# A smaller cap on the bytes of the first loads, and one weight piece finished by halves

## The chip, the cores and the metric

The kernel runs on one core of one Trainium2 chip. The number that counts is the device time of one execution in microseconds (us), as a median over runs. In the text PE is TensorE, DVE is VectorE, ACT is ScalarE, POOL is GpSimd and SP is SyncE, which here only starts DMA transfers. "PEq", "SPq" and so on are the sequencers of these engines.

## The reference

Two steps are computed, one behind the other. The first is a retention layer: for 8 batches and 8 heads, with 576 positions and a head dimension of 64, the scores are multiplied by a decay and a causal mask, with no softmax. The second is a feed-forward block over the 4608 tokens, 512 to 2048 to 512, with a PReLU between.

```python
scores = scale * np.matmul(q, k.transpose(0, 1, 3, 2))
Dmat = np.where(rel >= 0, gamma[:, None, None] ** rel[None, :, :], 0.0)
attn = np.matmul(scores * Dmat[None], v)          # (8, 8, 576, 64)
x = attn.transpose(0, 2, 1, 3).reshape(4608, 512)
h = x @ w_in                                      # (4608, 2048)
g = np.maximum(h, 0.0) + alpha * np.minimum(h, 0.0)
out = (g @ w_out).astype(np.float32)
```

q, k and v are 4-byte floats in HBM. The two weight matrices lie there as 8-byte floats, because they are multiplied by a double when they are set up; each is 1M elements, 8 MB. The kernel turns them into 4-byte floats itself.

## The kernel before, in words

**Blocks.** The feed-forward block works on blocks of 256 tokens (18 of them, numbered kb) and 8 units i of 256 hidden columns. A unit first makes ph = w_in' x (PE, `plain_unit` L419 for the first two blocks, `mlp_unit` L463 for the others), then the activation g (ACT and DVE), then adds g w_out to the sums po (PE, L398 and L381). The first two blocks (`PLAIN`) use plain products, while the weights are still arriving; the other 16 use a scheme with seven products in the place of eight.

**Weights.** Each weight matrix comes in 16 pieces of 512 KB, in the order two of w_in, two of w_out, two of w_in and so on (`pieces`). In `fetch` a piece of w_in is loaded by two DMAs of 256 KB, a piece of w_out by one of 512 KB, through `load` on SP's queue (L78). `piece_in` (L285) starts the conversion on ACT: `a` is the absolute value of the upper halves (L296), and the lower halves are scaled in place (L298). `piece_out` (L301) ends it: three DVE operations on 128x512 elements, clamp (L307), shift and mask (L310), sign (L312), and one POOL operation that adds the lower halves (L314).

**The cap.** `load` keeps a list of the loads asked for so far. A load waits until an earlier one has landed, chosen so that the bytes asked for after that one, with its own, come to at least `in_flight[0]`. The value is 5 << 18 (five times 256 KB, 1.25 MB) at the beginning and 7 << 18 after part one of the first batch has been asked for; later it is 0, which is no cap. SP takes its DMAs in order, so a load that waits holds all behind it.

**The first batch.** Batch 0 goes in three parts of 4, 4 and 1 chunks of 64 positions (`PARTS`). Part 0 is six transfers of 256 KB: k, q and v, each in two halves; its q goes over ACT's queue and isn't counted by the cap (L161). `part_transposes` (PE L697), `part_scores` (PE L716, DVE L723), `part_states` (PE L736, ACT L744, POOL L746) and `part_values` (PE L764 and L775) make the first 256 columns of x; three ACT copies for each half of them (L781, L783) bring them into `xb[0]`, and after those the first unit can start. All this is written out by hand, one call after the other, in a scheduling scope that keeps the order on each engine:

```python
fetch(6)
load_part(1)
in_flight[0] = 7 << 18
fetch(8)
...
piece_in(1)
part_states(0)
piece_in(2)
piece_out(2)
part_carry(0)
part_values(0)
...
piece_in(2)
piece_out(1)
part_scale(1, 1)
plain_unit(0, 0)
```

So on ACT the conversion of pieces 0, 1 and 2 (numbered from 0; piece 2 is the first of w_out) stands ahead of the copies into `xb[0]`. The steps below call the loads k0, k1, v0, v1 (part 0), w0 to w7 (the pieces, with a and b for two halves), k0' to v1' (part 1). The first unit's 16 matmul instructions go through the four blocks of 128 columns of x, cc = 0 to 3: cc 0 and 1 need piece 0, cc 2 and 3 need piece 1.

Of the kernel before, what the change touches and what calls it, by code (L numbers as in the profile page):

```python
# [10 lines left out]
FP32 = mybir.dt.float32  # L11
INT32 = mybir.dt.int32
UINT32 = mybir.dt.uint32
ACTF = mybir.ActivationFunctionType
ALU = mybir.AluOpType
# [3 lines left out]
def kernel(  # L19
# [10 lines left out]
    nc = tc.nc  # L30
# [3 lines left out]
    P = 128  # L34
# [9 lines left out]
    HM = DM // 2  # L44
# [42 lines left out]
                ahead += n  # L87
            flight.append((ins, size))

    in_flight = [5 << 18]  # L90

# [99 lines left out]
    for i in range(NBIT - 1):  # L193
        nc.vector.scalar_tensor_tensor(out=dif[:, i + 1], in0=dif[:, i], scalar=2.0,
                                       in1=dif[:, i], op0=ALU.add, op1=ALU.mult)
# [6 lines left out]
                            op=ALU.mult)  # L202
    nc.vector.tensor_scalar(pf, pf, 1.0, None, ALU.add)

    for o, x, y in ((slice(0, 2), slice(0, 2), slice(3, 5)), (0, 0, 1), (0, 0, 2), (1, 0, 5)):
# [7 lines left out]
                                   in1=pf[:, 6], op0=ALU.mult, op1=ALU.mult)  # L213
# [17 lines left out]
    for h2 in range(2):  # L231
# [6 lines left out]
                                       in1=tabx[hd, :, 0], op0=ALU.add, op1=ALU.mult)  # L238
# [13 lines left out]
    HI_MAX = float(np.array([0x47EFFFFF], np.uint32).view(np.float32)[0])  # L252
    HI_MIN = float(np.array([0x38000000], np.uint32).view(np.float32)[0])
# [10 lines left out]
    def fetch(n):  # L264
        while npiece[0] < min(n, len(pieces)):
            srcs, at = pieces[npiece[0]][0], npiece[0]
            npiece[0] += 1
            free[:] = [t for t in free if at < gone.get(t, len(pieces))]
            t = free.pop(0)
            if isinstance(t, str):  # L270
                raw = ring.tile([P, 4 * HM], INT32, tag=t, name=f"raw_{at}")
            else:
                raw = w_in[t][:, 4:6].rearrange("p s u c f -> p (s u c f)").bitcast(INT32)
            for i, src in enumerate(srcs):
                to = raw
                if len(srcs) > 1:
                    to = raw.rearrange("p (x e f two) -> p x e f two", x=2, e=2, two=2)[:, :, i]
                load(to, src, P * 4 * HM * 4 // len(srcs))
            raws.append((raw, t))
# [21 lines left out]
    def piece_out(n):  # L301
        for _ in range(min(n, len(half_done))):
            at, a, lo, hi, t = half_done.pop(0)
            dst = pieces[at][1]

            c = ps_h.tile([P, 2, HM], INT32, tag="psh1", name=f"wc_{at}")
            nc.vector.tensor_scalar(c.bitcast(FP32), a, HI_MIN, HI_MAX, ALU.max, ALU.min)  # L307


            nc.vector.tensor_scalar(c, c, 3, 0x3FFFFFF8,  # L310
                                    ALU.logical_shift_left, ALU.bitwise_and)
            nc.vector.scalar_tensor_tensor(out=dst.bitcast(INT32), in0=hi, scalar=-0x40000000,  # L312
                                           in1=c, op0=ALU.bitwise_and, op1=ALU.bitwise_or)
            nc.gpsimd.tensor_tensor(out=dst.bitcast(INT32), in0=dst.bitcast(INT32), in1=lo,  # L314
                                    op=ALU.add)
            free.append(t)
            fetch(at + 1 + AHEAD)

# [517 lines left out]
# [5 lines that stand above are left out]
    aps = ps_a.tile([P, NFC], FP32, tag="psa", name="aps")  # L841
    nc.tensor.transpose(aps, a16, ident[0:NFC, 0:NFC])
    piece_out(1)
    nc.vector.tensor_copy(alpha, aps)
    nc.vector.tensor_scalar(nalpha, alpha, -1.0, None, ALU.mult)
# [4 lines that stand above are left out]
# [97 lines left out]
    for b in range(2, B):  # L947


        nq, first, at = len(queue), b * NPAIR, {}  # L950
# [56 lines left out]
```

## Time and profile before

| | |
|---|---|
| time, median of 3 runs | 1020.53 us (1019.59 to 1022.61) |
| span of the profiled execution | 1018.5 us |
| PE busy | 1001.3 us, 98% |
| PE weight loads busy | 894.2 us, 88% |
| DVE, ACT, POOL busy | 778.3, 269.4, 179.2 us |
| first matmul of the first unit | 19.26 us after the start of the span |
| DMA share in the first 25 us | 9 tenths of all 16 engines |

PE works without a rest from the second slice of 25 us to the end, so a time that PE loses or wins near the start is found again at the end of the span. The first slice is the only one in which PE is busy for 6 tenths only, and the only one with a granted clock under 9 tenths. The change touches only what happens there. In the views that follow, an entry such as "[0.76 <-POOL w_in L314]" says how long the engine was idle before the entry and what released it.

### The profile page before, as it was taken

To read this page: it belongs to the slowest core of one execution; us is meant where nothing else is said; L and a number is where in the kernel's file an instruction comes from. 1 tells how busy PE (TensorE), PEld (TensorE's weight loads), DVE (VectorE), ACT (ScalarE), POOL (GpSimd) and SP (SyncE) were. 2 spreads that over 40 slices of the span, in tenths; PEclk is the share of its full clock that TensorE was granted. 3 is DMA by queue.
4 is the path that set the end of the run, shared out by engine and by line. 5 is a ranking of instruction groups with operands and counts; after the bars stand their busy time and mean duration, and the time that the engine had idled before them with its cause. 6 is when DMAs were issued, how large, how long until landed. Compare 5 with 4: busy or idle time off the path is not lost.

```text
span 1018.5 us, 23084 instructions
## 1 busy us (share of the span) xinstructions
PE 1001.3 (98%) x9385; PEld 894.2 (88%) x9385; DVE 778.3 (76%) x2086; ACT 269.4 (26%) x605; POOL 179.2 (18%) x201
## 2 busy tenths in 40 slices
PE   6999999999999999999999999999999999999997
PEld 5666668899999999999999999999999999999997
DVE  6669966878887888768778788887878777667665
ACT  4556653223222222122021312232222211000000
POOL 5656674300100020100010000200020001010000
PEclk8999999999999999999999999999999999999999
DMA  9975744322231323112112313222313000000000
GB/s 238 238 194 140 185 74 103 60 60 48 52 64 40 63 37 69 25 45 48 44 25 56 60 45 60 57 48 54 62 45 60 13 23 1 22 1 21 2 21 22
DMA packets 229308, 64.30 MB, mean 63 GB/s; under 512 B 214337, under 2 KB 222545, under 8 KB 229201
## 3 DMA queue, kind: packets, MB, share of 16 engines
q1 hardware_dynamic: 227088, 62.29, 27.1%
q8 instruction: 74, 1.21, 0.5%
q10 hardware_dynamic: 2112, 0.53, 0.3%
q14 instruction: 34, 0.27, 0.1%
HBM read 53.35 MB, written 9.44 MB: 62 GB/s over the span
## 4 chain that ended last, share of the span: by engine, by line
PE 94%; DVE 3%; DMA 1%; ACT 0%; issue 0%; SPq 0%; POOL 0%; DVEq 0%; ACTq 0%
PE ph L463 38%; PE po L381 37%; PE ph L419 6%; PE po L398 6%; PE pv L656 3%; PE ps L614 1%; PE ps L620 1%; DMA w_out<-in_k_dram 1%; PE ph L614 1%; DVE su L589 0%; DVE g L476 0%; PE pt L697 0%; DVE mt L636 0%; PE ps L716 0%; PE ps L556 0%
## 5 line engine op out<-in xcount | busy, mean ns | idle before, releaser
L381 PE MATMUL po<-w_out,g 128*128 128x256 f32 x1792 | 410.9, 381 | 0.2
L381 PEld LDWEIGHTS po<-w_out,g 128*128 128x128 f32 x1792 | 330.1, 190 | 42.7 <-DVE g L487 1.3
L476 DVE TENSOR_TENSOR g<-ph,g 128x256 f32<-128x256 f32 (+1 forms) x512 | 187.0, 386 | 127.2 <-ACT g L471 75.2
L463 PE MATMUL ph<-xb,w_in 128*128 128x128 f32 x2048 | 272.7, 276 | 0.0
L463 PEld LDWEIGHTS ph<-xb,w_in 128*128 128x128 f32 x2048 | 257.1, 192 | 7.9 <-issue 0.7
L463 PE MATMUL ph<-xt,w_in 128*128 128x128 f32 x1536 | 213.8, 275 | 0.7 <-DVE g L476 0.7
L463 PEld LDWEIGHTS ph<-xt,w_in 128*128 128x128 f32 x1536 | 192.2, 192 | 1.1 <-PE ph L463 0.8
L487 DVE TENSOR_TENSOR g<-g 128x128 f32<-128x128 f32 x512 | 127.2, 289 | 5.4
L471 ACT COPY g<-ph 128x128 f32<-128x128 f32 x128 | 34.1, 266 | 327.7 <-PE ph L463 217.1
L528 POOL TENSOR_TENSOR qx<-qx,tabx 128x576 f32<-128x576 f32 x28 | 32.3, 1153 | 379.6 <-DMA qx<-in_q_dram 223.4
L481 DVE SCALAR_TENSOR_TENSOR g<-g 128x512 f32<-128x512 f32 x128 | 91.3, 714 | 3.8
L479 DVE TENSOR_SCALAR g<-g,alpha 128x256 f32<-128x256 f32 x256 | 84.3, 370 | 2.8
L597 ACT COPY vn<-su 64x512 f32<-64x512 f32 x56 | 34.6, 617 | 135.2 <-DVE su L591 134.5
L419 PE MATMUL ph<-xb,w_in 128*128 128x256 f32 x256 | 61.7, 397 | 0.8 <-POOL w_in L314 0.8
L419 PEld LDWEIGHTS ph<-xb,w_in 128*128 128x128 f32 x256 | 50.1, 198 | 11.0 <-issue 2.4
L398 PE MATMUL po<-w_out,g 128*128 128x512 f32 x128 | 58.6, 599 | 0.9 <-DVE g L435 0.9
L625 DVE SCALAR_TENSOR_TENSOR mt<-ph,th,mask 64x64 f32<-64x64 f32 x48 | 13.6, 283 | 52.5 <-PE ph L614 52.2
L665 ACT COPY xb<-pv 128x256 f32<-128x256 f32 (+3 forms) x84 | 22.7, 321 | 109.8 <-PE pv L656 109.8
L636 DVE SCALAR_TENSOR_TENSOR mt<-ps,th,mask 64x256 f32<-64x256 f32 x96 | 46.1, 481 | 2.3
L533 ACT ACTIVATE vn<-vn,tabv 64x576 f32<-64x576 f32 x56 | 43.3, 774 | 8.7 <-DMA vn<-in_v_dram 7.8
L398 PEld LDWEIGHTS po<-w_out,g 128*128 128x128 f32 x128 | 23.4, 190 | 24.5 <-issue 22.9
L589 DVE SCALAR_TENSOR_TENSOR su<-su,gch 128x64 f32<-128x64 f32 x84 | 43.1, 513 | 2.1
(134 smaller groups left out, 717.0 us busy)
## 6 DMA issues: line engine op xcount, KB each, us to landing
out_dram<-osb SPq DMA_DIRECT2D x36, 256.0 KB, 2.3
kx<-in_k_dram SPq DMA_DIRECT2D x112, 72.0 KB, 2.6
qx<-in_q_dram SPq DMA_DIRECT2D x112, 72.0 KB, 3.0
vn<-in_v_dram SPq DMA_DIRECT2D x56, 144.0 KB, 3.2
kn<-in_k_dram SPq DMA_DIRECT2D x56, 144.0 KB, 3.3
raw<-in_moe_w_in_dram SPq DMA_DIRECT2D x24, 256.0 KB, 4.5
raw<-in_moe_w_out_dram SPq DMA_DIRECT2D x10, 512.0 KB, 5.4
w_in<-in_moe_w_out_dram SPq DMA_DIRECT2D x6, 512.0 KB, 5.7
```

Of the source, the lines that this page charges most:

```text
L381: nc.tensor.matmul(acc[kb][n // 2][:, n % 2, :], g[:, x, :], w_out[i][:, y, :], start=(i == 0 and n % 2 == 0), stop=(i == NU - 1 and (n % ...
L398: nc.tensor.matmul(acc[kb][m], g[:, 2 * x + m], w_out[i][:, 2 * x:2 * x + 2].rearrange("p x f -> p (x f)"), start=(i == 0 and x == 0), sto ...
L419: nc.tensor.matmul(ph[:, x], w_in[i // UST][:, cc // 2 * 2 + x, i % UST, cc % 2], xb[kb][:, cc], start=(cc == 0 and x == 0), stop=(cc == N ...
L463: nc.tensor.matmul(ph[m][:, o], w_in[i // UST][:, l, i % UST, cc], r[:, cc], start=(n in (0, 3) and cc == 0), stop=(n in (2, 6) and cc == ...
L476: nc.vector.tensor_tensor(out=o, in0=x0, in1=x1, op=ALU.add)
L479: nc.vector.tensor_scalar(g[:, 4 + 2 * m:6 + 2 * m], g[:, 2 * m:2 * m + 2], 0.0, alpha[:, fc:fc + 1], ALU.min, ALU.mult)
L481: nc.vector.scalar_tensor_tensor(out=g[:, 0:4].rearrange("p x t -> p (x t)"), in0=g[:, 0:4].rearrange("p x t -> p (x t)"), scalar=0.0, in1 ...
L487: ins = nc.vector.tensor_tensor(out=g[:, o, :], in0=g[:, x0, :], in1=g[:, x1, :], op=op)
L533: nc.scalar.activation(vn[x, h2], vn[x, h2], ACTF.Copy, scale=tabv[x, c:c + 1])
L589: nc.vector.scalar_tensor_tensor(out=su[:, j], in0=su[:, j - 2], scalar=g2, in1=su[:, j], op0=ALU.mult, op1=ALU.add)
L597: nc.scalar.copy(vn[half(h2), h2, 1:], su[half(h2)])
L636: nc.vector.scalar_tensor_tensor(out=mt[to, h2, p2:NJ - 1:2], in0=ps[p2][half(x), 0], scalar=th[to, 3, h:h + 1], in1=mask[to, None, :].to_ ...
```

## The change

Two edits. The first makes the cap smaller while the first two parts of q, k and v and pieces 0 to 5 are asked for: 0.75 MB in the place of 1.25 MB; from piece 6 and part 2 on the cap is 1.75 MB as before. It is for having less queued in the DMA engines at the time when the first matmuls run. The second edit lets `piece_out` finish piece 1 in two halves of columns (cc = 2, then cc = 3), so that the first half's POOL addition does not wait for the second half's DVE work.

```diff
-    in_flight = [5 << 18]
+    in_flight = [3 << 18]
...
-            nc.vector.tensor_scalar(c.bitcast(FP32), a, HI_MIN, HI_MAX, ALU.max, ALU.min)
...
-            nc.vector.tensor_scalar(c, c, 3, 0x3FFFFFF8,
-                                    ALU.logical_shift_left, ALU.bitwise_and)
-            nc.vector.scalar_tensor_tensor(out=dst.bitcast(INT32), in0=hi, scalar=-0x40000000,
-                                           in1=c, op0=ALU.bitwise_and, op1=ALU.bitwise_or)
-            nc.gpsimd.tensor_tensor(out=dst.bitcast(INT32), in0=dst.bitcast(INT32), in1=lo,
-                                    op=ALU.add)
+            for f in (slice(0, P), slice(P, HM)) if at == 1 else (slice(0, HM),):
+                dst_e, c_e, a_e, hi_e, lo_e = [y[:, :, f] for y in (dst, c, a, hi, lo)]
...
+                nc.vector.tensor_scalar(c_e.bitcast(FP32), a_e, HI_MIN, HI_MAX, ALU.max, ALU.min)
...
+                nc.vector.tensor_scalar(c_e, c_e, 3, 0x3FFFFFF8,
+                                        ALU.logical_shift_left, ALU.bitwise_and)
+                nc.vector.scalar_tensor_tensor(out=dst_e.bitcast(INT32), in0=hi_e,
+                                               scalar=-0x40000000, in1=c_e,
+                                               op0=ALU.bitwise_and, op1=ALU.bitwise_or)
+                nc.gpsimd.tensor_tensor(out=dst_e.bitcast(INT32), in0=dst_e.bitcast(INT32),
+                                        in1=lo_e, op=ALU.add)
```

The order of the instructions on every engine stays as it was, but for three more on DVE and one more on POOL in piece 1; in the first unit PE gets a wait of its own ahead of cc = 3.

## The prediction, before the changed kernel ran

> **What bounds the kernel now.** I read the page first: busy shares, slices, the chain that ended last.
>
> ```profile
> PE   6999999999999999999999999999999999999997
> PEclk8999999999999999999999999999999999999999
> PE 94%; DVE 3%; DMA 1%; ACT 0%; issue 0%; SPq 0%; POOL 0%; DVEq 0%; ACTq 0%
> ```
>
> PE is 94% of the chain and full from slice 2 on. What the change can give is the distance by which the first dense unit ends earlier, if PE then finds its next inputs. So I read PE, ACT and SP over the first 30 us (start, duration, engine and line, idle before and its releaser).
>
> ```profile
> 12.90 0.33 PE L764 MATMUL pv<-pa,w_out 64*64 64x64 f32 x2
> 13.50 1.15 PE L764 MATMUL pv<-pa,w_out 64*64 64x64 f32 x62 [0.27 <-DVE pa L723]
> 14.58 0.42 PE L775 MATMUL pv<-pT,w_out 64*32 64x64 f32 x14
> 17.13 1.21 PE L775 MATMUL pv<-pT,w_out 64*32 64x64 f32 x82 [2.13 <-issue]
> 19.26 6.74 PE L419 MATMUL ph<-xb,w_in 128*128 128x256 f32 x16 [0.76 <-POOL w_in L314]
> ```
>
> Two things cost PE time here. In the middle of one group of L775, with no new operand, PE stands for 2.13 us and nothing released it ("issue"). And the first unit takes 6.74 us, where a later one of 16 takes 3.45 us in the chain of waits (58.89, 65.78). The windows view shows why (busy times, then the clock as the third number from the end):
>
> ```profile
> 11.80:18.60 6.80, 4.29 (x237) 3.65 (x230) 6.06 (x10) 5.30 (x12) 4.16 (x5) 1.00 0.94 303
> 18.60:25.40 6.80, 6.14 (x15) 4.92 (x16) 3.72 (x7) 3.95 (x9) 4.58 (x5) 0.50 0.99 233
> ```
>
> The trace's clock record: full from 11.79, half from 18.62, full from 25.45.
>
> The releaser named for the first unit is piece 1's POOL addition (17.89 to 19.17). But cc 0 and 1 need piece 0, done at 17.31, and xb, whose first half ACT finishes at 18.37 + 0.74 = 19.11. ACT's copies bind:
>
> ```profile
> 15.28 0.67 ACT L296 ACTIVATE wa<-w_in 128x512 f32<-128x512 f32 x1
> 15.84 0.66 ACT L298 ACTIVATE w_in<-w_in 128x512 int32<-128x512 uint32 x1
> 17.96 0.37 ACT L781 COPY xb<-pv 128x256 f32<-128x256 f32 x1 [1.47 <-PE pv L775]
> 18.37 0.74 ACT L783 COPY xb<-pv 64x256 f32<-64x256 f32 x2
> ```
>
> ACT is free at 16.50 and waits 1.47 us for PE's delayed L775. So the "issue" gap sets the start.
>
> **What the gap is.** PE's instruction records stop at number 449, and again at 1217 for 0.76 us in the same line. The difference is 768. The DMA packets of q8 (74 of 16,384 bytes, 1.21 MB, PE's instructions by their number) show one at 14.79 lasting 0.96, then PE goes on 1.38 us after its end; one at 38.08 lasting 1.02, PE on at 40.59, 1.49 us after it. [...] If the request comes on entering the block before (instruction 193, about 12.1 us; 961, about 34.2), the fetch waited 2.7 us under the cap of 1.25 MB and 3.8 us under 1.75 MB before its packet started.
>
> [...] those of 4096 bytes take about 0.18 us, those of 1024 about 0.05. [...] A wait behind all that is queued fits both fetches: 1.25 MB at some 300 GB/s is 4.2 us; less about 1.1 us from issue to first byte (k0: 0.80 to 1.91) [...], 2.3 are left; for 1.75 MB, 3.9. Both are near the observed waits, though the request times are inferred.
>
> **The cap's part.** For 0.75 MB the same sum is 2.6 - 1.9 = 0.7 us, at most 1.5 where two 512 KB loads overlap. From the packet records, whose 4-byte packets are semaphore writes, I take the landings before: k0 4.04, k1 6.32, v0 8.30, v1 9.49, w0a 10.44, w0b 11.19, w1a 11.94, w1b 12.69, w2 14.79, w3 16.74, k1' 22.6, q0' 23.7, q1' 24.7, v1' 27.4. SP answers a landing in 0.56 us:
>
> ```profile
> 11.00 0.35 SPq L78 DMA_DIRECT2D w_in<-in_moe_w_out_dram  x1
> 12.50 0.35 SPq L78 DMA_DIRECT2D raw<-in_moe_w_out_dram  x1
> 13.20 3.27 SPq L78 DMA_DIRECT2D raw<-in_moe_w_in_dram  x4
> ```
>
> With 0.75 MB: v1 waits for k0, and its first byte, 4.04 + 0.56 + 1.1 = 5.7, is still ahead of its turn at 8.08: no loss. w0a waits for k1, w0b for v0 (8.30 + 1.66 = 9.96, turn at 10.21): no loss. w1a waits for v1: 11.15 against 10.96. w1b: about 12.1, landed 13.1 against 12.69; ACT takes it at 14.05: no cost. w2 waits for w1a (landed 12.15): first byte 13.8, 1.5 us for 512 KB at 350 GB/s, landed about 15.9, 1.1 later than before.
>
> PE: at 12.1 only w1 is under way, so the instruction block arrives before 14.8 or within 0.7 us of it. The remaining 82 instructions need POOL's sums (14.49, 15.26), so L775 ends near 16.3 in the place of 18.34.
>
> ACT: its activation for piece 2 now waits for w2, 15.9 for 15.28, and with both activations done (1.22 us by the rows) is at 17.15. The first half of xb then takes 0.37 + 0.74 and is there at 18.25. The first unit starts at about 18.4, 0.86 us earlier. So of the 2.13 us of the gap, less than half comes through; the new wait for w2 takes the rest.
>
> **The clock.** [...] 25.45 - 18.62 is 6.83, [...] I estimate that the half clock costs about 1.7 us after (3.4 us at half) against 2.5 before (5 us), 0.8 less. The first unit would then end 0.86 + 0.8 = 1.7 us earlier.
>
> **What later loads take.** Part 1 goes three loads at a time and lands later by my count: k1' 23.7, q0' 25.0, q1' 26.2, v1' 28.8. Needed before at: k' 25.84 (L697), q' 24.53 (POOL L677), transposes of q' 29.58, v' 31.48. With 1.7 us less, k' is in time (24.1), q' scaled by 27.2 against 27.9: in time. v' in time (29.8). Nothing is lost up to some 2 us.
>
> **The halves.** DVE: three operations of 0.69 to 0.70 us become six on 128x256; nearest rows L479 0.370 and L435 0.476 (128x256), so 1.2 for each half, 2.4 against 2.16. The first addition on POOL then runs at once after piece 0's (17.31 to about 18.0; L746 at this size 0.73), the second ends near 18.75 in the place of 19.17. PE reaches cc 2 at 18.4 + 1.7 (eight at full clock), and the second half of xb is there at 19.4. So the halves are worth nothing unless the unit starts before 17.5; their 0.25 us on DVE lies beside PE's first unit. Zero.
>
> Sum: 1020.5 - 1.7 = 1018.8.
>
> **Rivals.** B: the clock never drops, because PE stands for 2.1 us between 16.3 and 18.4 and no longer for 2.1 and 0.8. The first unit then ends at 22.0, 4.0 us earlier, but k1' (23.7), q1' (26.2) and the v' scaling hold PE back; 2.5 to 4 us are left: about 1017. For it: fewer gaps; against: 63% of 11.79 to 18.62 was busy when it dropped, about 64% after. C: the fetch does not depend on the bytes queued; L775 starts at 17.13 as before and the time is 1020.3, less nothing but noise. For it: the request times are inferred, [...]. D, on the slow side: loads one by one leave the DMA engines idle (0.75 MB per 1.1 + 0.8 + 0.56 us and the transfer is 246 GB/s, where 1 KB packets ran at 350), so w2, part 1 and piece 6 come 2 to 4 us later than counted and PE waits for them: 1024. Against: k, q and v move at only 220 GB/s, which three in flight can still feed.
>
> **Numbers.** Mine 0.44, B 0.28, C 0.18, D 0.10. Faster by over 0.3% (3.06 us, under 1017.5) is most of B and the edge of mine: 0.28. Slower is D: 0.10. Within: 0.62. The range leaves out D and the far end of B: 1015.8 to 1021.4.
>
> **What would show it.** Right: the idle "issue" before L775 falls under 0.7 us; ACT's L296 on piece 2 waits for a DMA; the first L419 starts at 18 to 18.7; windows show the half clock for 3 to 4 us of the unit. Wrong: an unchanged 2.1 us gap (C); L697 or L677 waiting for part 1 for over 1 us (D); a first unit of 3.6 us (B).

## The result, and the profile after

| | before | after |
|---|---|---|
| median | 1019.78 us (6 runs, 1019.16 to 1022.61) | 1025.32 us (6 runs, 1023.50 to 1026.99) |
| ratio | | 1.0052, 95% interval 1.0036 to 1.0067 |
| span of the profiled execution | 1018.5 us | 1021.8 us |

The change costs half a per cent, some 5.3 us. The profiled execution after is the fastest of its six, so its trace shows 3.3 us of it. PE's timeline of the changed kernel over the first 38 us (start, duration, operation, idle before and releaser; lines behind L314 have moved on by four, so L775 is L779 here and L419 is L423):

```profile
14.40 0.42 PE L779 MATMUL pv<-pT,w_out 64*32 64x64 f32 x14
16.57 1.21 PE L779 MATMUL pv<-pT,w_out 64*32 64x64 f32 x82 [1.76 <-issue]
17.71 0.23 PE L846 MATMUL aps<-ident,a 16*128 16x16 f32 x1
19.95 6.17 PE L423 MATMUL ph<-xb,w_in 128*128 128x256 f32 x16 [2.01 <-POOL w_out L756]
27.39 0.63 PE L701 MATMUL pt<-ident,w_out 128*128 128x128 f32 x4 [1.27 <-DMA w_out<-in_k_dram]
28.44 0.63 PE L701 MATMUL pt<-ident,w_out 128*128 128x128 f32 x4 [0.42 <-DMA w_out<-in_k_dram]
...
31.66 0.66 PE L701 MATMUL pt<-ident,w_out 128*128 128x128 f32 x4 [0.43 <-POOL w_out L681]
...
37.74 3.29 PE L423 MATMUL ph<-xb,w_in 128*128 128x256 f32 x14 [1.06 <-issue]
```

The gap named "issue" before L779 is still there, 1.76 us for 2.13. The first unit starts 0.69 us later, not earlier. Then come waits that the kernel before doesn't have: twice for part 1's k, once for part 1's q (the POOL scaling L681 ahead of the transposes waits for its DMA), and a new "issue" gap in the middle of a unit.

What releases the first unit is named as a POOL operation, 19.31 to 19.92, that writes another tensor; ACT's copies into the block of x tell more:

```profile
17.58 0.67 ACT L296 ACTIVATE wa<-w_in 128x512 f32<-128x512 f32 x1 [1.44 <-DMA w_in<-in_moe_w_out_dram]
18.15 0.65 ACT L298 ACTIVATE w_in<-w_in 128x512 int32<-128x512 uint32 x1
18.70 0.35 ACT L785 COPY xb<-pv 128x256 f32<-128x256 f32 x1
19.06 0.74 ACT L787 COPY xb<-pv 64x256 f32<-64x256 f32 x2
```

Before, ACT waited for PE here; now it stands 1.44 us for w2's DMA, while the operands of its copies have been ready since PE's L779 ended at 17.78. The first half of x is there at 19.80, and the unit's first weight load follows 0.12 us later, as it did before (19.11 and 19.23).

The windows view shows what stands behind the DMA waits, in its last two columns (share of the 16 DMA engines, GB/s). The kernel before, then after:

```profile
10.00:20.00 10.00, 6.83 (x292) 6.02 (x292) 8.12 (x13) 6.68 (x16) 6.64 (x8) 0.93 0.96 308
20.00:30.00 10.00, 9.09 (x32) 6.61 (x31) 5.12 (x11) 5.82 (x11) 4.61 (x4) 0.73 1.00 256
```

```profile
10.00:20.00 10.00, 5.96 (x292) 5.17 (x290) 7.68 (x14) 5.91 (x14) 6.73 (x9) 0.91 0.67 213
20.00:30.00 10.00, 8.31 (x27) 6.14 (x28) 6.00 (x12) 5.96 (x12) 3.25 (x3) 0.75 0.78 193
```

Over these 20 us the DMA engines move 1.58 MB less (10 us times 95 and 63 GB/s), which at the 290 GB/s of the following 16 us is 5.4 us of loading. SP's own waits say who stops it: 17.6 us of waits for DMA in the first 40 us, where the kernel before had 8.2. The chain that ended last is made of it:

```profile
4.79 5.43 DMA w_out<-in_v_dram
10.24 3.87 DMA raw<-in_moe_w_in_dram
14.13 3.43 DMA w_in<-in_moe_w_out_dram
17.57 4.83 DMA raw<-in_moe_w_in_dram
22.44 0.03 issue
22.47 3.57 DMA raw<-in_moe_w_in_dram
26.05 3.23 DMA w_out<-in_q_dram
```

From 0.80 to 29 us the last finished work is load after load, each asked for when an earlier one had landed. In the kernel before the same stretch of the chain was one DMA up to 7.1 us, and then PE, DVE and POOL.

**Where the time goes, by PE's instructions.** I compared the start of the n-th weight load of PE (counted from 0) in the two traces:

```
n of the weight load      208    225    310    340    500    700   1700   9384
start before, us        14.58  17.14  21.10  30.24  38.07  46.35  174.86 1012.77
after minus before, us  -0.18  -0.55  +0.69  +1.69  +3.02  +3.09  +3.09  +3.30
```

All but 0.2 us is lost by 46 us; the rest of the program only carries it along.

### The profile page after: what moved, and what is told of

Its sections match the earlier page's. It is cut to its first block, busy times and chain, and to the rows that moved or that the text cites. A ratio compares the mean times of both kernels' runs of the same rounds, so it can differ in the third digit from the quotient of the medians.

```text
span 1021.8 us, 23090 instructions
## 1 busy us (share of the span) xinstructions
PE 1001.6 (98%) x9385; PEld 893.6 (87%) x9385; DVE 779.9 (76%) x2089; ACT 269.2 (26%) x605; POOL 179.2 (18%) x202
## 4 chain that ended last, share of the span: by engine, by line
PE 92%; DMA 3%; DVE 3%; ACT 0%; issue 0%; POOL 0%; SPq 0%; DVEq 0%; ACTq 0%; POOLq 0%
PE ph L467 38%; PE po L385 37%; PE po L402 5%; PE ph L423 5%; PE pv L660 3%; DMA raw<-in_moe_w_in_dram 1%; PE ps L618 1%; PE ps L624 1%; DMA w_out<-in_v_dram 1%; PE ph L618 1%; DVE su L593 0%; DVE g L480 0%; DMA w_out<-in_k_dram 0%; DVE mt L640 0%; DMA w_in<-in_moe_w_out_dram 0%
## 5 line engine op out<-in xcount | busy, mean ns | idle before, releaser
L385 PEld LDWEIGHTS po<-w_out,g 128*128 128x128 f32 x1792 | 330.2, 190 | 42.8 <-DVE g L491 1.5
L423 PE MATMUL ph<-xb,w_in 128*128 128x256 f32 x256 | 61.4, 395 | 3.1 <-POOL w_out L756 2.0
L423 PEld LDWEIGHTS ph<-xb,w_in 128*128 128x128 f32 x256 | 49.6, 197 | 13.4 <-issue 3.9
L669 ACT COPY xb<-pv 128x256 f32<-128x256 f32 (+3 forms) x84 | 22.6, 321 | 109.4 <-PE pv L660 109.4
L453 POOL TENSOR_TENSOR xt<-xb 128x256 f32<-128x256 f32 x16 | 11.6, 728 | 186.9 <-PE ph L467 186.9
```

Of the source, the lines that this page charges most:

```text
L385: nc.tensor.matmul(acc[kb][n // 2][:, n % 2, :], g[:, x, :], w_out[i][:, y, :], start=(i == 0 and n % 2 == 0), stop=(i == NU - 1 and (n % ...
L423: nc.tensor.matmul(ph[:, x], w_in[i // UST][:, cc // 2 * 2 + x, i % UST, cc % 2], xb[kb][:, cc], start=(cc == 0 and x == 0), stop=(cc == N ...
```

## The experiments

Ten kernels were run, each beside runs of the kernel before on the same chip; ratios are to those. The traces are compared further down. Three of them are of executions 2.4 to 3.0 us above their kernel's median: that of the late cap (1025.38 us), of w2 held (1022.94) and of 2.25 MB after w2 (1023.50).

**Which of the two edits costs.** The cap alone:

```diff
-    in_flight = [5 << 18]
+    in_flight = [3 << 18]
```

> The cap of 0.75 MB alone; piece 1 in one go as before. Theory 1 (three loads leave the DMA engines idle between loads, so pieces 2 to 6 and part 1 land 2 to 5 us later and PE waits for them): as slow as the changed kernel, 1023.5 to 1027, ratio 1.004 to 1.007. Theory 2 (the halves' three extra DVE operations and the extra POOL one are what costs): within 1 us of before, 1019 to 1021. Theory 3 (half the loss from each): about 1022.5.

Measured: 1024.18 us for 1019.14, ratio 1.0054 (1.0038 to 1.0071). The halves alone, with the cap at 1.25 MB:

```diff
+            for f in (slice(0, P), slice(P, HM)) if at == 1 else (slice(0, HM),):
```

> The halves of piece 1 alone; the cap stays at 1.25 MB. Theory 1: no difference, 1019 to 1021, since the first unit starts on the ACT copies and not on piece 1. Theory 2: 1023 to 1027. Theory 3: about 1022.5.

Measured: 1019.36 us, ratio 1.0004 (0.9996 to 1.0011). So the cap is the whole of it, and the halves are nothing within 0.1%.

**Other caps.** 1 MB and 2.25 MB, no halves:

```diff
-    in_flight = [5 << 18]
+    in_flight = [4 << 18]      # the other run: [9 << 18]
```

> A cap of 1 MB, no halves. Theory 1: between the two, 1020 to 1023, with part 1's second k half landing at 23.5 to 26 (22.6 with 1.25 MB, 27.6 with 0.75 MB). If the loss is of another kind than a graded delay of the loads, it stays at 1019 to 1020 or jumps to 1025.

> A cap of 2.25 MB, no halves. Theory 1 alone: loads no later than before, so 1018 to 1020. If PE's instruction block waits behind every byte queued at its request, it now waits behind w2 and w3 and not only w2: its packet starts at 16 to 17 in the place of 14.79, the gap in L775 grows from 2.1 to 3.3 to 4.3 us, the first unit starts 1 to 2 us later, and the time is 1020.5 to 1022. If the fetch doesn't depend on the bytes queued, the gap stays at 2.1.

Measured: 1 MB 1020.81 us, ratio 1.0021 (1.0013 to 1.0029), with part 1's second k half at 24.5; 2.25 MB 1019.46 us, ratio 1.0006 (0.9998 to 1.0014). The loss is graded with the cap, as the theory of late loads has it. With 2.25 MB the gap is longer, though less than expected (2.90 us, packet at 15.58), and the first unit starts 1.2 us later. By 46 us PE is 0.2 us ahead again, and not because it waits less for data: 0.5 us comes back in the first unit, more of which runs at full clock (6.25 us for 6.74), and 0.9 us around 40 us, where the kernel before has another "issue" gap of 0.76 us and this one has none, as that instruction block's packet starts at 36.05 for 38.08. PE's timeline of the run with 2.25 MB:

```profile
14.68 0.42 PE L775 MATMUL pv<-pT,w_out 64*32 64x64 f32 x14
18.00 1.49 PE L775 MATMUL pv<-pT,w_out 64*32 64x64 f32 x82 [2.90 <-issue]
```

**First loads or later ones.** The small cap only up to piece 1, and only from piece 2 on:

```diff
-    in_flight = [5 << 18]
+    in_flight = [3 << 18]
...
+    fetch(2)
+    in_flight[0] = 5 << 18     # the other run: 5 first, 3 here
     fetch(6)
     load_part(1)
```

> The cap of 0.75 MB only for part 0 and pieces 0 and 1, then 1.25 MB for pieces 2 to 5 and part 1; no halves. If the loss of the changed kernel comes from part 1 and pieces 3 to 6 landing late, most of it is gone: part 1's second k half lands at 23 to 25 and the time is 1019 to 1021. If it comes from pieces 0 to 2 landing late (the first unit's start), it stays at 1023 to 1025. In both cases PE's instruction block should wait behind w2 again (packet at about 15.5, gap in L775 over 2.5 us).

> The complement: 1.25 MB for part 0 and pieces 0 and 1, 0.75 MB for pieces 2 to 5 and part 1; no halves. If late part 1 is the loss: part 1's second k half at 25 to 27, time 1022 to 1024. If the first pieces are the loss: 1019 to 1020. The instruction block should wait only for w1b, landing near 12.7, so the gap in L775 falls to 0.6 us or less.

Measured: early 1020.55 us, ratio 1.0009 (1.0001 to 1.0017); late 1022.36 us, ratio 1.0034 (1.0023 to 1.0044), part 1's second k half at 23.8 and at 26.1. So most of the loss belongs to pieces 2 to 5 and part 1. One thing came out otherwise in the early run: the instruction block waited for w1b, not w2 (packet at 13.59). In the late run the gap before L775 nearly goes, and the first unit is still no earlier than 19.05 (the last row is cut at 22 us):

```profile
14.45 0.42 PE L775 MATMUL pv<-pT,w_out 64*32 64x64 f32 x14
15.04 1.21 PE L775 MATMUL pv<-pT,w_out 64*32 64x64 f32 x82 [0.17 <-issue]
16.18 0.23 PE L844 MATMUL aps<-ident,a 16*128 16x16 f32 x1
19.05 3.14 PE L419 MATMUL ph<-xb,w_in 128*128 128x256 f32 x7 [2.63 <-POOL w_in L314]
```

**The instruction block by itself.** The cap stays at 1.25 MB, but w2 waits until w1b has landed:

```diff
+    fetch(2)
+    in_flight[0] = 1 << 18
+    fetch(3)
+    in_flight[0] = 5 << 18
     fetch(6)
     load_part(1)
```

> The cap of 1.25 MB throughout, but w2 alone waits until w1b has landed; no halves. If the instruction block waits behind every byte queued at its request, it now waits for w1b only: its packet starts at 12.5 to 13.0 in the place of 14.3 to 14.8, the gap in L775 falls from 2 us to 0.6 or less, while w2 lands near 16.3 and keeps ACT until 17.5, so the first unit starts at 18.5 to 19.0 and the time is 1018.5 to 1020. If the fetch doesn't depend on the queue, the gap stays near 2 us and the time rises to 1020 to 1021.

Measured: the packet of the instruction block starts at 12.57, and the gap is gone. But w2 lands at 16.3, the first unit starts at 19.09, and the time is 1020.49 us, ratio 1.0018 (1.0009 to 1.0027). In this trace a later instruction block costs more than the first one did: its packet starts at 33.75 (31.16 before), and PE stands 3.35 us at the instruction where the kernel before has no gap.

```profile
14.66 1.68 PE L775 MATMUL pv<-pT,w_out 64*32 64x64 f32 x96
19.09 5.38 PE L419 MATMUL ph<-xb,w_in 128*128 128x256 f32 x16 [2.59 <-ACT xb L783]
...
36.85 4.78 PE L419 MATMUL ph<-xb,w_in 128*128 128x256 f32 x14 [3.35 <-issue]
```

**Taking ACT's wait for w2 away as well**, with piece 1 by halves:

```diff
-    piece_in(2)
+    piece_in(1)
     piece_out(2)
     part_carry(0)
     part_values(0)
+    piece_in(1)
```

> As the run that holds w2, with two more edits: ACT converts piece 2 after the copies into the first block of x and not before them, and piece 1 is finished by halves. If ACT's wait for w2 is what swallows the shorter gap, the first unit now starts at 17.4 to 17.9, and the time is 1016.5 to 1018.5, the best of all; part 1's second k half, near 24.3, then begins to hold PE after the first unit. If something else holds the unit (piece 1, the sums), it starts at 18.5 or later and the time is 1018.5 to 1020.

Measured: 1020.92 us, ratio 1.0015 (1.0007 to 1.0023). The shorter way to the first unit works, the time doesn't follow. PE's timeline of this run:

```profile
14.76 1.92 PE L779 MATMUL pv<-pT,w_out 64*32 64x64 f32 x96
16.61 0.23 PE L851 MATMUL aps<-ident,a 16*128 16x16 f32 x1
18.08 3.72 PE L423 MATMUL ph<-xb,w_in 128*128 128x256 f32 x16 [1.24 <-POOL w_in L318]
24.36 0.63 PE L701 MATMUL pt<-ident,w_out 128*128 128x128 f32 x4 [2.56 <-DMA w_out<-in_k_dram]
```

No gap, the clock doesn't drop in this trace before 1016.8 us, the unit takes 3.72 us for 6.74 and ends at 21.8, over 4 us earlier. Then PE stands 2.56 us for part 1's k, and 0.63 and 1.09 us in "issue" gaps ahead of 34.12 and 40.32, for 0.76 us in all before. At weight load 700 it is 0.27 us ahead of the kernel before, and nothing is left of that at the end.

**Loading part 1's k earlier, and asking for more at a time.** Two tries at a version that beats both:

```diff
...
+    once.append(5 << 18)       # 1 << 18 holds for the first of these loads alone
+    load_part(1, (0,))
+    fetch(4)
+    load_part(1, (1,))
     fetch(6)
-    load_part(1)
+    load_part(1, (2,))
...                             # and ACT's order of the pieces
```

> Built on the run with w2 held and ACT's order changed: part 1's k is now loaded ahead of w2 and w3, its q ahead of w4 and w5 (the hold behind w1b is on the first of these k loads), and ACT converts piece 4 after the first unit's activation. If after the earlier start of the first unit only the late k and q of part 1 held PE, k lands by 17.5 and q by 23, the waits of PE's L701 group for DMA vanish, and PE stands 1.5 to 3 us ahead of the kernel before at 60 us: 1016.5 to 1018.5. If it is the total of bytes that counts, the later pieces (4 to 6) hold PE in their place and the time stays at 1019.5 to 1021.

```diff
-    in_flight[0] = 5 << 18
+    in_flight[0] = 9 << 18     # after w2, and in the place of 7 << 18
```

> As the run with w2 held and ACT's order changed, but 2.25 MB after w2, and for piece 6 and on. If what holds PE after the first unit is that part 1 is asked for too late, its second k half lands 0.5 to 1.2 us earlier (near 23.5) and the time falls by as much, to 1019 to 1020.5. If the later instruction blocks wait behind more queued bytes, the gaps named issue between 30 and 42 us grow by 0.5 to 2 us and the time is 1020.5 to 1022.

Measured: 1020.72 us, ratio 1.0018 (1.0010 to 1.0026), and 1020.68 us, ratio 1.0026 (1.0017 to 1.0035). With k first the waits for k vanish and the first unit starts at 17.31, but ACT now waits 2.67 us for w2 and 1.45 us for w4, and PE 2.54 and 2.09 us for DVE's work behind these:

```profile
20.98 0.67 ACT L299 ACTIVATE wa<-w_in 128x512 f32<-128x512 f32 x1 [2.67 <-DMA w_in<-in_moe_w_out_dram]
23.98 0.66 PE L704 MATMUL pt<-ident,w_out 128*128 128x128 f32 x4 [2.54 <-DVE alpha L858]
26.72 3.75 PE L405 MATMUL po<-w_out,g 128*128 128x512 f32 x4 [2.09 <-DVE g L442]
```

So the waits have moved to the loads put behind. And a second thing costs time: in both traces the clock is at half from 25.3 or 25.4 to 32.1 or 32.2 us, after PE had waited, and four matmuls of L405 take 3.75 us for 1.96. What k first would bring with the clock at full isn't shown. With 2.25 MB the second k half lands at 26.7 and not near 23.5, and SP's instruction for the load after it took 4.17 us in this trace; why isn't known, and that run says little of its question. No kernel here was faster than the one before.

**All of them side by side.** From the packet records and PE's timelines, in us; "block" is the start of the instruction block's packet, "behind" the load that was landing when it started, or had just landed (first to last of its 16 semaphore writes), "gap" the idle time before the second part of the L775 group:

| kernel | behind | block | gap | first unit | k1' landed | ratio |
|---|---|---|---|---|---|---|
| before | w2, 13.74 to 14.79 | 14.79 | 2.13 | 19.26 | 22.6 | |
| halves alone | w2, to 14.28 | 14.28 | 1.83 | 18.73 | 23.2 | 1.0004 |
| 2.25 MB | w4a, 15.43 to 16.14 (w3 to 15.39) | 15.58 | 2.90 | 20.42 | 21.3 | 1.0006 |
| 1 MB | w1b, to 13.62 | 13.62 | 1.29 | 19.14 | 24.5 | 1.0021 |
| 0.75 MB early | w1b, 13.34 to 14.78 | 13.59 | 1.62 | 19.51 | 23.8 | 1.0009 |
| 0.75 MB late | w1b, to 12.58 | 12.58 | 0.17 | 19.05 | 26.1 | 1.0034 |
| w2 held | w1b, to 12.63 | 12.57 | none | 19.09 | 24.4 | 1.0018 |
| 0.75 MB alone | w1b, to 14.26 | 14.26 | 1.49 | 19.76 | 27.4 | 1.0054 |
| changed kernel | w1b, 13.42 to 14.47 | 14.30 | 1.76 | 19.95 | 27.6 | 1.0052 |

Among the kernels that differ in the cap alone, the ratio rises with the landing of k1' from 22.6 on, and the start of the first unit says little.

## Why the prediction was wrong, step by step

**What bounds.** Right: the gap is PE's instruction block. In the traces before and after PE has 18,968 records (9,385 matmuls, as many weight loads, 198 of its sequencer) and queue q8 74 packets, so 256.3 records for each; and from the ninth packet on, each started between 3.2 us before and 1.6 us after PE began the record that stands 256 before the block's first one (number 193 for the block that begins at 449). PE came to instruction 193 at 11.6 to 12.2 us in the nine kernels of the table, and the packet started within the semaphore writes of one load or 0.01 us behind them; in seven of the nine it started 3 to 4 ns after one such write had ended. That is a wait behind the loads queued before it, as the prediction supposed. It overtook only loads asked for less than a microsecond before that, or later (w2 in the early run, asked at 11.46 with PE at 193 at 11.68; w4b with 2.25 MB, 11.28 and 12.12). In the changed kernel w2 was asked for only at 14.13, and with w1b (rows of 1 KB) the last load ahead of the block it was 2.5 us from instruction 193 (11.84) to the packet (14.30); when this first block is asked for is still inferred. Of the 1.9 us that the prediction's sum takes off, 1.1 are k0's from asking to the first byte; the other 0.8, for the landing, were an estimate of mine (they stand in rival D's sum too) and weren't shown: in the changed kernel w1b's last row ended at 14.46 and its last semaphore write at 14.47. And an instruction block cost PE up to 3.35 us here (w2 held).

**The cap's part, where it failed.** The step that failed is the time of one 256 KB load from asking to landing, which the sum took as if it didn't depend on how many loads are in flight: 1.1 us to the first byte, 0.75 us of transfer at the 350 GB/s of five in flight, and 0.24 us to land, 2.1 in all. Measured in the changed kernel, with three in flight: w1a asked at 10.24, landed at 13.42, 3.2 us; w4a 17.58 to 20.68, 3.1; k0' 23.14 to 26.57, 3.4 (2.7 to 4.2 over its fourteen loads of this size from w0a on). Their first bytes came 1.4 to 1.6 us after asking, and w0a, w0b, w1a and w1b took 1.70, 1.33, 1.22 and 1.52 us from the first byte to the last. With SP's answer (some 0.4 to 0.9 us) a load goes round in about 3.7 us, and three of 256 KB in flight are 212 GB/s, the 213 and 193 of the windows.

The packets themselves were no slower. Those of 1 KB took 53 ns on average between 10.55 and 11.85 us, at 204 GB/s, and 51 ns in the kernel before between 10.25 and 12.25 us, at 348 GB/s; but 10.5 packets were under way at a time for 17.6. So the DMA engines stood partly idle (share 0.67 in that stretch); why three loads don't fill them isn't shown. All that follows from the sum was too early: w1b 13.1, measured 14.47; w2 15.9, measured 17.22; k1' 23.7, measured 27.61; q1' 26.2, measured 30.13; v1' 28.8, measured 32.56.

**PE and the block.** Expected: the block before 14.8, or within 0.7 us of it. Measured: a gap of 1.76 us. The wait behind w1b was as supposed and its input was wrong: w1b, still ahead of the block, landed at 14.47 and not at 13.1. A smaller queue that drains more slowly left the block nearly where it was (14.30 for 14.79).

**ACT.** The new wait for w2 was foreseen (1.44 us by the trace), but w2 landed at 17.22 and not at 15.9. ACT came to the copies at 18.70 and not at 17.15, though PE's L779 had ended at 17.78, and the unit starts at 19.95 and not at 18.4.

**The clock.** Expected: half clock for 3.4 us, against 5 before; both were estimates of mine. The trace before has 6.83 us (18.62 to 25.45), 6.19 of them in the unit. In the profiled run after it lasted from 18.15 to 24.97, 6.8 us again; the unit began 1.8 us after the drop (19.95), and PE was busy for 1.61 us of the first 3.41 and for all of the second. In the 0.75 MB run without halves it lasted 3.4 us, from 19.39 to 22.80, and that saved nothing: PE waited 2.23 us for k in the place of 1.27. How busy PE was in the first 3.41 us at half differs: 89% in that run and 83% with the late cap (from 18.45), where the half clock then ended; 81% before (from 18.62) and 79% with 2.25 MB (from 18.77), where it went on. The busy share alone doesn't tell when the clock drops in these traces, so the argument against rival B was weak: in the run with w2 held and ACT's order changed it stayed at full over 6.83 us that were 56% busy (20.10 to 26.93), and in the late run it dropped after 6.83 us of 72% (38.93 to 45.76).

**What later loads take.** Expected: nothing up to 2 us. Measured: +1.0 us between weight loads 310 and 340 (k, q), and +1.3 up to 500. In the latter the "issue" gap of 1.06 us is again an instruction block: its packet starts at 35.23, where w6 has landed at 35.22, six microseconds later than in the kernel before.

**The halves.** Zero, as predicted. On DVE they took 0.43, 0.43 and 0.42 us for each half, 2.6 us in all for an estimate of 2.4.

**The rivals.** It went as rival D, whose sum (0.75 MB in 3.2 us, 246 GB/s) was nearer to the 213 than that of the main case, and which I gave one chance in ten. The argument against it was that k, q and v move at 220 GB/s, which three in flight can feed. That came true and missed the point. Part 0 landed as before (v1 at 9.51 for 9.49), with its q, which the cap doesn't count, beside the three; and from k0' to v1' it was 6.0 us after and 6.2 before. The delay arose in the pieces between them: w0a was 0.1 us later than before, w1b 1.8, w3 3.0, w5b 5.5, and k0' 5.4.

**Open.** The profile shows 3.3 us, the medians differ by 5.5. In the traces of the late cap and of the held w2 the clock dropped a second time for 3.4 us, at 45.76 and at 36.49, after PE had waited. Such a drop in the slower executions of the changed kernel could be a part of the rest, but their mean clocks don't put them in order (1026.62 us at 0.996 of full, 1025.28 us at 0.994), and no trace of one was taken. So some 2 us stay without a cause.

## What to carry to other kernels

The cap on bytes in flight was a cap on the rate here (from 10 to 20 us 213 GB/s with 0.75 MB, 308 with 1.25 MB): divide it by the whole round of one load in that state, from asking through landing to the answer of the queue (3.7 us here), and compare with the rate the stage needs, which this program had at 308 GB/s before the change. A transfer time taken with five loads in flight (0.75 us for 256 KB) must not be used for three (1.22 to 1.70 us). And where a stage is bound by the arrival of a fixed number of bytes, removing a stall early in it only moves PE up to the next late load: here 4 us won at 22 us were down to 0.3 at 46 us.

## What was not expected of the hardware

PE's instruction blocks waited behind the data loads, in step with what was queued: the packet of the first one started at 12.57 with w1b the last load ahead and at 15.58 with w3 landed and w4a landing. What was queued at about the time when PE came to a new block of 256 instructions went with stalls of 0 to 3.35 us, and a lower rate of loads moved a later block behind another load (35.23 for 31.16).

Three loads of 256 KB in flight moved at some 204 GB/s where five moved at 348, with packets nearly as quick as before (53 and 51 ns for 1 KB): fewer of them were under way. A load of 256 KB (rows of 256 bytes) with nothing queued ahead of it took 2.4 us from asking to landing (part 1's first k half in the run with k first, 13.15 to 15.58), for 2.7 to 4.2 us as one of three in the changed kernel. The weight pieces lost time under the smaller cap (w5b landed 5.5 us later); part 1's k, q and v, which move at some 220 GB/s, lost none of their own (6.0 us from the first landing to the last for 6.2).
